# A fused attention and MLP kernel: a shorter attention pipeline, the first layer started one tick earlier, and the softmax multiply on another engine

## The chip, the cores and the metric

The kernel runs on one core of one Trainium2 chip. The metric is device microseconds (us) of one execution; the time before is the median of three runs. A core has TensorE (PE: matmuls and transposes, with PEld for its weight loads), VectorE (DVE), ScalarE (ACT), GpSimd (POOL) and SyncE (SP, which here issues most of the DMAs). Each engine works through its own queue in order, and semaphores order the engines among each other.

## The reference

Three parts follow one another on 2304 tokens of width 512:

```
scores = (q_c @ k_c.T) / sqrt(64)             # chunks of 64 tokens, 8 heads of 64
attn   = exp(scores - max); attn /= sum(attn) + 1e-9
x = attn @ v_c                                # 2304 x 512
h = relu(x @ w_in); x = (h * h) @ w_out       # 512 -> 2048 -> 512, w_in, w_out in float64
p = domain_probs / (sum + 1e-9)
out = sum over 4 experts of p[e] * (relu(x @ w1[e]) @ w2[e])   # 512 -> 1024 -> 512
```

## The kernel before

The 2304 tokens are 18 tiles of 128, two chunks of attention each. The first layer pair (`l1`: x @ w_in, `l2`: @ w_out) works on five blocks of 384, 384, 512, 512 and 512 tokens, in four passes over 512 hidden columns each; a step m is one pass, one block and one group of 128 hidden columns, 80 steps in all. Each step is 12 matmuls of `l1` (line 301) and 12 of `l2` (line 333) of the step before; each product is made of three, from a high and a low part of both operands.

The order of the work is written out by hand (`tc.manual_schedule()`): what the program text issues first stands first in its engine's queue. One loop runs over ticks r. In tick r the step of the first layer is m = r - LEAD. The first ticks also carry attention, one tile at several stages:

- `s0` of tile r+1: four transposes each of q and k (line 221), copied out of PSUM by ACT (line 225).
- `s1` of tile r: 32 small matmuls for the scores (line 236); DVE then takes the maximum and subtracts it (lines 242, 243).
- `exp` of tile r on ACT (line 249), `norm` of tile r-1 on DVE: sum, add, reciprocal (lines 254 to 256) and the multiply that normalises (line 257).
- `s2` of tile r-LAG_A: four transposes of the normalised scores (line 263), copied by ACT (line 265).
- `s3` of tile r-LAG_A: 32 small matmuls with v (line 277), written out as a high part by ACT (line 284) and a low part by DVE (line 285).

PE's queue in a tick of the attention is: `s1`, nine matmuls of `l1`, `s2`, `s0` of q, three of `l1` and three of `l2`, `s0` of k, three of `l2`, `s3`, the last six of `l2`. In ticks before LEAD the matmuls of the layers are absent. Between the matmuls of a step stand a relu on ACT (line 311), a squaring on DVE (line 312), and the split of the result (ACT line 316, DVE line 317).

The weights w_in and w_out arrive as 64-bit data and are converted on the way, one unit of 128x512 at a time: `unit_convert` is ACT (lines 128, 129), DVE (130, 133, and later in the tick 138, 141), and then POOL (142, 143); `unit_split` is ACT (154) and POOL (155). `FIRST` names the tick at which each of the first eight units is converted; it is loaded two ticks earlier and split one tick later. These are POOL's only instructions in the attention. SP issues at the start of tick r the loads of q and k of tile r+2, parts of v, and units of weights.

The scores of one tile live in `e`, of which there are LAG_A + 1 buffers. x of the first block is complete when `s3` of tile 2 is written out; the first `l1` reads it.

Of the kernel before, what the change touches and what calls it, by code (L numbers as in the profile page):

```python
# [13 lines left out]
ALU = mybir.AluOpType  # L14
# [4 lines left out]
P = 128  # L19
CH = 64  # L20
# [2 lines left out]
LAG = 1  # L23
RING_A = 4
RING_B = 4
LEAD = 5
QK_BUFS = 3
ACC_EARLY = 3
FIRST = [0, 1, 2, 3, 4, 5, 6, 7]
WARM = 8  # L30
SECOND = [-3, -2, -1, 1, 2, 3, 4, 5]
RAW_BUFS = 4
# [1 line left out]
HALF = 384  # L34
NSUP = 3
SWAP = 63
LAG_A = 2
UOFF = [1, 3, 5, 7, 9, 11, 13, 15]


# [5 lines left out]
def tile_kernel(ctx, tc, q, k, v, moe_w_in, moe_w_out, moe2_p, moe2_w1, moe2_w2, out):  # L46
    nc = tc.nc
    B, H, S, D = q.shape
# [5 lines left out]
    NTILE = NT // P  # L54
# [161 lines left out]
    def s0_stage(t, tags, which):  # L216
        nm, dst = (("q", qT), ("k", kT))[which]
        a = qkv.pop((nm, t))
        pt = bank(tags).rearrange("p (j s) -> p j s", j=HX)
        for j in range(HX):  # L220
            nc.tensor.transpose(  # L221
                out=pt[:, j, :], in_=a[:, 2 * j:2 * j + 2].rearrange("p x d -> p (x d)"), identity=ident
            )
        o = qkp.tile([P, HX, P], F32, tag=nm + "T", name=nm + "T")
        nc.scalar.copy(o, pt)
        dst[t] = o

    def s1_stage(t, tags):
        qt, kt = qT.pop(t), kT.pop(t)
        pt = [bank(tags)[:, :HX * CH].rearrange("p (j k) -> p j k", j=HX) for _ in range(2)]  # L230
        for c in range(2):
            cs = slice(c * CH, (c + 1) * CH)
            for j in range(HX):
                for x in range(2):
                    r = slice(x * CH, (x + 1) * CH)
                    nc.tensor.matmul(  # L236
                        pt[x][cs, j, :], lhsT=qt[r, j, cs], rhs=kt[r, j, cs], start=True, stop=True
                    )
        e = qkp.tile([P, HX, 2, CH], F32, tag="e", name="e", bufs=LAG_A + 1)
        mx = qkp.tile([P, 2, HX, 1], F32, tag="mx", name="mx")  # L240
        for x in range(2):
            nc.vector.tensor_reduce(out=mx[:, x], in_=pt[x], axis=AX.X, op=ALU.max)
            nc.vector.tensor_tensor(
                out=e[:, :, x, :], in0=pt[x], in1=mx[:, x].to_broadcast([P, HX, CH]), op=ALU.subtract
            )
        et[t] = e

    def exp_stage(t):
        nc.scalar.activation(out=et[t], in_=et[t], func=AF.Exp, scale=scale)

    def norm_stage(t):
        e = et[t].rearrange("p j x k -> p (j x) k")
        sm = qkp.tile([P, H, 1], F32, tag="sm", name="sm")
        nc.vector.tensor_reduce(out=sm, in_=e, axis=AX.X, op=ALU.add)
        nc.vector.tensor_scalar_add(sm, sm, 1e-9)
        nc.vector.reciprocal(sm, sm)
        nc.vector.tensor_tensor(out=e, in0=e, in1=sm.to_broadcast([P, H, CH]), op=ALU.mult)

    def s2_stage(t, tags):
        e = et.pop(t).rearrange("p j x k -> p j (x k)")  # L260
# [60 lines left out]
    def l2(i):  # L321
        p, tb, f = steps[i]
        T = BLOCKS[tb]
        bh, bl = halves[p * G + f, 1]
        hi, lo = gh.pop(i), gl.pop(i)
        for d in range(KD):
            ds = slice(d * P, (d + 1) * P)
            if f == 0:
                pacc[d] = bank("a")
            o = pacc[d][:, :T]  # L330
            prods = ((bh[:, ds], hi[:, :T]), (bh[:, ds], lo[:, :T]), (bl[:, ds], hi[:, :T]))
            for n, (w, y) in enumerate(prods):
                nc.tensor.matmul(  # L333
                    o, lhsT=w, rhs=y, start=(f == 0 and n == 0), stop=(f == G - 1 and n == 2)
                )
            if f == G - 1:
                evacuate(p, tb, d)
            yield
# [27 lines left out]
    for sp in range(NSUP):  # L366
        if sp < NSUP - 1:
            r = [starts[2 * sp] + i * P for i in range(3)] + [starts[2 * sp + 1] + i * P for i in range(3)]
        else:
            r = [starts[NB - 1] + i * P for i in range(3)] + [starts[2 + i] + HALF for i in range(3)]  # L370
# [200 lines left out]
    def at(tick, kind, fn, *args):  # L571
        jobs[kind].setdefault(max(0, tick), []).append((fn, args))

    def do(tick, kind):
        return [fn(*args) for fn, args in jobs[kind].pop(tick, ())]
# [11 lines left out]
    for p in range(npass1):  # L587
        for u, (f, which) in enumerate(order):
            if p == 0:
                tick = FIRST[u]  # L590
            elif p == 1:
                tick = NTILE + LAG_A + SECOND[u]
            else:
                tick = LEAD + (p - 1) * G * NB + UOFF[u]
            unit = (p * G + f, which)
            if tick > 1:
                at(tick - 2, "load", unit_load_later, *unit)
            at(tick, "convert", unit_convert, *unit)
            at(max(tick + 1, NTILE + LAG_A if p == 1 else 0), "split", unit_split, *unit)
    def run_all(loads):  # L600
        for y in loads:
            if hasattr(y, "__next__"):
                for _ in y:
                    pass

    with tc.manual_schedule():
# [27 lines left out]
        def mlp(m):  # L634
            if 0 <= m < NS:
                first = l1(m)
                for _ in range(KD):
                    yield next(first)
            second = l2(m - LAG) if 0 <= m - LAG else iter(((),) * KD)
            if r < NTILE + LAG_A:  # L640
                yield next(second)
            yield next(second)
            if 0 <= m < NS:
                for _ in first:
                    pass
            yield from second

        def run(chunks, n=None):
            while n is None or n > 0:
                try:  # L650
                    next(chunks)
                except StopIteration:
                    return
                n = None if n is None else n - 1
# [3 lines left out]
            SWAP: [(w1_load, (0,)), (w1_load, (1,)), (w2_load, (0,))],  # L658
            LEAD + NS - 4: [(w1_split, (0, 0)), (w1_split, (0, 1)), (w1_load, (2,))],
        }  # L660
        for i in range(4):
            early[SWAP + 5 + i] = [(w1_add, (0, i))]
            early[LEAD + NS - 8 + i] = [(w1_add, (1, i))]
        y0_at = LEAD + (npass1 - 1) * G * NB + 2 * G + LAG

        for which in range(2):
            s0_stage(0, "ttthaaaa", which)
        for r in range(LEAD + NS + LAG):
            m = r - LEAD
            tags = "ttthaaaa" if m < 0 else "t"  # L670
            ch = mlp(m) if m >= 0 else iter(())
            if r == NTILE + LAG_A:
                att.close()
                late["x"] = ctx.enter_context(tc.tile_pool(name="xq", bufs=1, side="right"))
                late["w"] = lw.enter_context(tc.tile_pool(name="wpb", bufs=RING_B, side="right"))
            run_all(do(r, "load"))
            if r < NTILE + LAG_A:
                if r < NTILE:
                    s1_stage(r, tags)
                if 0 <= r - 1 < NTILE:  # L680
                    norm_stage(r - 1)
                conv = do(r, "convert")
                for c in conv:
                    next(c)
                run(ch, 3)
                if 0 <= r - LAG_A:
                    s2_stage(r - LAG_A, tags)
                if r + 1 < NTILE:
                    s0_stage(r + 1, tags, 0)
                run(ch, 2)  # L690
                if r + 1 < NTILE:
                    s0_stage(r + 1, tags, 1)
                for c in conv:
                    run(c)
                run(ch, 1)
                if 0 <= r - LAG_A:
                    s3_stage(r - LAG_A, tags)
                if r < NTILE:
                    exp_stage(r)
                do(r, "split")  # L700
            else:
                if r == SWAP:
                    staging.close()
                    late["raw"] = ctx.enter_context(tc.tile_pool(name="raw", bufs=1, reuse_waits="tile"))
                for fn, args in early.pop(r, ()):
                    fn(*args)
                if r > y0_at:
                    next(late.setdefault("y0", y_combine(0)), None)
                if m < NS:
                    run(ch, KD + 2)  # L710
                    conv = do(r, "convert")
                    for c in conv:
                        next(c)
                    run(ch, 1)
                    for c in conv:
                        run(c)
                    do(r, "split")
            if m < NS:
                run(ch)
# [68 lines left out]
```

## Time and profile before

| what | us |
|---|---|
| median of 3 runs | 1249.46 (1248.11 to 1249.78) |
| span of the profiled execution, first to last instruction | 1246.2 |
| between span and median of the runs | 3.3 |
| PE busy | 1228.4 (99% of the span) |
| DVE busy | 687.5 (55%) |
| ACT busy | 522.7 (42%) |
| POOL busy | 621.7 (50%) |

The page gives the span of the profiled execution but no time of its own for it; the 3.3 us that the runs lie above the span are taken as what lies around it. In the page's strip of 40 slices of 31 us, PE stands at 7 and 8 tenths in the first two and at 9 or more in all others but the last; the granted TensorE clock (PEclk) is at 7 and 8 in the same two and at 9 after. Attention lasts until about 160 us of the span.

### The profile page before, as it was taken

What the parts mean: (1) busy time and instruction counts of PE and PEld (TensorE: products, weight loads), DVE (VectorE), ACT (ScalarE), POOL (GpSimd) and SP (SyncE); (2) the same over time, 40 slices, a digit from 0 to 9 for tenths busy, and PEclk for the clock granted to TensorE, in tenths of its full rate; (3) what the DMA queues carried; (4) which work ended last, traced back from release to release, by engine and by line L of the source; (5) the groups of instructions that cost most, each with busy time, mean ns of one, the idle gap of its engine ahead of it and who ended that gap; (6) DMA issues with size and microseconds to landing.
All of it is one profiled execution on the core that took longest, in us unless ns stands there. A gap on an engine that the chain in (4) does not pass through costs nothing.

```text
span 1246.2 us, 18128 instructions
## 1 busy us (share of the span) xinstructions
PE 1228.4 (99%) x7048; PEld 1088.0 (87%) x7048; DVE 687.5 (55%) x1135; ACT 522.7 (42%) x934; POOL 621.7 (50%) x507
## 2 busy tenths in 40 slices
PE   7899999999999999999999999999999999999998
PEld 6788889889889988888888888888888888888887
DVE  6966757555563445355555573555555735555555
ACT  5654555333432234533333355333333553333331
POOL 3510146421431023766766686767766866666650
PEclk7899999999999999999999999999999999999999
DMA  9855022210101000322222223222222132222211
GB/s 208 191 128 137 19 68 85 52 51 18 52 1 51 1 1 20 99 68 68 68 68 68 68 76 111 68 69 68 67 68 67 63 120 69 66 68 65 68 35 62
DMA packets 137253, 87.19 MB, mean 70 GB/s; under 512 B 63184, under 2 KB 120528, under 8 KB 137168
## 3 DMA queue, kind: packets, MB, share of 16 engines
q1 hardware_dynamic: 134544, 85.39, 25.1%
q8 instruction: 55, 0.90, 0.3%
q10 hardware_dynamic: 2624, 0.66, 0.3%
q14 instruction: 30, 0.25, 0.1%
HBM read 81.30 MB, written 4.72 MB: 69 GB/s over the span
## 4 chain that ended last, share of the span: by engine, by line
PE 94%; DVE 3%; DMA 1%; ACT 1%; issue 0%; SPq 0%; DVEq 0%; ACTq 0%
PE psa L548 32%; PE pst L503 24%; PE psa L333 15%; PE pst L301 9%; PE psh L301 6%; PE psh L503 4%; PE pst L277 1%; PE pst L221 1%; PE pst L236 1%; DMA q<-in_q 1%; DMA k<-in_k 1%; PE pst L263 0%; DVE cv L130 0%; DVE cv L133 0%; DVE cv L138 0%
## 5 line engine op out<-in xcount | busy, mean ns | idle before, releaser
L548 PE MATMUL psa<-ar 128*128 128x512 f32 x1728 | 445.7, 393 | 0.0
L548 PEld LDWEIGHTS psa<-ar 128*128 128x128 f32 x1728 | 320.0, 188 | 50.3
L471 POOL TENSOR_TENSOR ar<-raw,ar 128x896 fp32r<-128x896 f32 x96 | 204.1, 2128 | 274.7 <-ACT ar L470 274.7
L503 PE MATMUL pst<-ar 128*128 128x384 f32 x1728 | 339.2, 335 | 0.9 <-ACT u L512 0.9
L503 PEld LDWEIGHTS pst<-ar 128*128 128x128 f32 x1728 | 307.3, 188 | 22.9 <-ACT u L512 1.6
L561 DVE SCALAR_TENSOR_TENSOR o<-psa,prob,o 128x512 f32<-128x512 f32 x270 | 201.5, 748 | 173.4 <-PE psa L548 173.4
L142 POOL TENSOR_TENSOR raw<-raw 128x512 f32<-128x512 f32 x32 | 33.3, 1041 | 228.3 <-issue 103.9
L461 POOL TENSOR_TENSOR raw<-raw 128x256 f32<-128x256 f32 x192 | 140.4, 750 | 8.4 <-DMA raw<-in_moe_w 4.8
L480 POOL TENSOR_TENSOR ar<-raw,ar 128x512 fp32r<-128x512 f32 x96 | 123.4, 1305 | 12.5 <-ACT ar L479 12.5
L512 ACT COPY u<-pst 128x384 f32<-128x384 f32 x96 | 46.0, 479 | 163.7 <-PE pst L503 163.7
L333 PE MATMUL psa<-ar 128*128 128x512 f32 (+1 forms) x480 | 112.8, 375 | 0.1
L516 ACT ACTIVATE ar<-pst 128x384 fp32r<-128x384 f32 x96 | 47.2, 492 | 149.7 <-DVE pst L537 116.3
L333 PEld LDWEIGHTS psa<-ar 128*128 128x128 f32 x480 | 86.3, 188 | 12.6 <-DVE ar L317 0.4
L333 PE MATMUL psa<-ar,h 128*128 128x512 f32 (+1 forms) x320 | 93.2, 372 | 1.1 <-ACT ar L316 0.8
L516 ACT ACTIVATE ar<-psh 128x384 fp32r<-128x384 f32 x96 | 47.2, 492 | 109.8 <-DVE psh L526 78.6
L470 ACT CAST ar<-raw 128x896 fp32r<-128x896 f32 x96 | 90.0, 939 | 0.0
L517 DVE SCALAR_TENSOR_TENSOR ar<-psh,ar 128x384 fp32r<-128x384 f32 x96 | 53.5, 558 | 53.6 <-ACT ar L516 53.6
L317 DVE TENSOR_TENSOR ar<-r,ar 128x512 fp32r<-128x512 f32 (+1 forms) x80 | 60.6, 757 | 39.4 <-ACT ar L316 37.8
L517 DVE SCALAR_TENSOR_TENSOR ar<-pst,ar 128x384 fp32r<-128x384 f32 x96 | 53.5, 557 | 31.2 <-ACT ar L516 29.1
L312 DVE SCALAR_TENSOR_TENSOR r<-pst,r 128x512 f32<-128x512 f32 (+1 forms) x48 | 30.7, 640 | 71.2 <-ACT r L311 71.2
L311 ACT ACTIVATE r<-pst 128x512 f32<-128x512 f32 (+1 forms) x48 | 26.7, 557 | 102.8 <-PE pst L301 102.1
L301 PE MATMUL pst<-ar,h 128*128 128x512 f32 (+1 forms) x240 | 69.3, 370 | 0.0
(107 smaller groups left out, 1514.9 us busy)
## 6 DMA issues: line engine op xcount, KB each, us to landing
raw<-in_moe_w SPq DMA_DIRECT2D x48, 512.0 KB, 3.8
raw<-in_moe_w SPq DMA_DIRECT2D x48, 256.0 KB, 3.0
raw<-in_moe_w SPq DMA_DIRECT2D x96, 128.0 KB, 3.1
raw<-in_moe_w_in SPq DMA_DIRECT2D x16, 512.0 KB, 3.9
raw<-in_moe_w_out SPq DMA_DIRECT2D x16, 512.0 KB, 3.7
out<-o SPq DMA_DIRECT2D x18, 256.0 KB, 3.2
q<-in_q SPq DMA_DIRECT2D x16, 256.0 KB, 4.5
k<-in_k SPq DMA_DIRECT2D x14, 256.0 KB, 5.0
```

The costliest lines, as they stand in the source:

```text
L301: nc.tensor.matmul(ph[:, :T], lhsT=w[:, kk, :], rhs=x[tb][:, kk, :], start=(kk == 0 and n == 0), stop=(kk == KD - 1 and n == 2),)
L317: nc.vector.tensor_tensor(out=lo[:, :T], in0=r[:, :T], in1=hi[:, :T].bitcast(F32), op=ALU.subtract)
L333: nc.tensor.matmul(o, lhsT=w, rhs=y, start=(f == 0 and n == 0), stop=(f == G - 1 and n == 2))
L461: nc.gpsimd.tensor_tensor(out=r[:, o], in0=r[:, a], in1=r[:, b], op=op)
L470: nc.scalar.copy(h, a)
L471: nc.gpsimd.tensor_tensor(out=l, in0=a, in1=h.bitcast(F32), op=ALU.subtract)
L480: nc.gpsimd.tensor_tensor(out=l, in0=a, in1=h.bitcast(F32), op=ALU.subtract)
L503: nc.tensor.matmul(p, lhsT=w[:, kk, :], rhs=y[:, kk, :], start=(kk == 0 and z == 0 and u in (0, 1, 3)), stop=(kk == 1 and z == 2 and u in ...
L516: nc.scalar.activation(out=h, in_=p, func=AF.Relu)
L517: nc.vector.scalar_tensor_tensor(out=l, in0=p, scalar=0.0, in1=h.bitcast(F32), op0=ALU.max, op1=ALU.subtract)
L548: nc.tensor.matmul(p, lhsT=w[:, ts], rhs=y[:, i, :], start=(i == 0 and z == 0), stop=(i == 1 and z == 2))
L561: nc.vector.scalar_tensor_tensor(out=o, in0=p, scalar=pe, in1=o, op0=ALU.mult, op1=ALU.add)
```

## The change

Five things change together. `LEAD` goes from 5 to 4, so step m runs in tick m+4. `LAG_A` goes from 2 to 1, so `s2` and `s3` handle the tile of the tick before, and `e` has two buffers in place of three. `norm` of tile r-1 is issued ahead of `s1` of tile r, and `exp` of tile r after the first half of the conversion rather than after `s3`. The normalising multiply is issued to POOL. In `FIRST` the last two units are converted in ticks 5 and 6 in place of 6 and 7, so that tick 5 converts two units.

```diff
-LEAD = 5
+LEAD = 4
-FIRST = [0, 1, 2, 3, 4, 5, 6, 7]
+FIRST = [0, 1, 2, 3, 4, 5, 5, 6]
-LAG_A = 2
+LAG_A = 1
@@ norm_stage
-        nc.vector.tensor_tensor(out=e, in0=e, in1=sm.to_broadcast([P, H, CH]), op=ALU.mult)
+        nc.gpsimd.tensor_tensor(out=e, in0=e, in1=sm.to_broadcast([P, H, CH]), op=ALU.mult)
@@ the loop over ticks, r < NTILE + LAG_A
+                if 0 <= r - 1 < NTILE:
+                    norm_stage(r - 1)
                 if r < NTILE:
                     s1_stage(r, tags)
-                if 0 <= r - 1 < NTILE:
-                    norm_stage(r - 1)
                 conv = do(r, "convert")
                 for c in conv:
                     next(c)
+                if r < NTILE:
+                    exp_stage(r)
                 run(ch, 3)
                 if 0 <= r - LAG_A:
                     s2_stage(r - LAG_A, tags)
...
                     s3_stage(r - LAG_A, tags)
-                if r < NTILE:
-                    exp_stage(r)
                 do(r, "split")
```

## Rows read from the trace of the kernel before

**Rows 1.** Windows: start:end, length, busy us (instructions) by engine, granted clock, DMA share, GB/s

```profile
10.00:20.00 10.00, 8.04 (x84) 6.22 (x84) 7.98 (x20) 6.78 (x12) 3.37 (x3) 0.50 1.17 222
30.00:40.00 10.00, 6.73 (x91) 5.67 (x87) 9.59 (x21) 6.38 (x13) 4.76 (x5) 0.66 0.99 219
40.00:50.00 10.00, 9.34 (x113) 8.53 (x113) 9.47 (x21) 7.30 (x14) 6.16 (x5) 1.00 0.86 205
```

**Rows 2.** Timeline of PE, 27 to 75 us: start, us, line, what [idle before, releaser]

```profile
27.88 0.63 PE L221 MATMUL psa<-ident,k 128*128 128x128 f32 x4 [0.69 <-DMA k<-in_k]
...
34.69 1.12 PE L221 MATMUL pst<-ident,k 128*128 128x128 f32 x4 [1.49 <-DMA k<-in_k]
...
39.23 2.19 PE L301 MATMUL psh<-ar 128*128 128x384 f32 x9 [0.17 <-DVE ar L285]
41.26 0.60 PE L263 MATMUL pst<-ident,e 128*128 128x128 f32 x4
...
46.91 0.60 PE L263 MATMUL pst<-ident,e 128*128 128x128 f32 x4
...
55.70 0.60 PE L263 MATMUL pst<-ident,e 128*128 128x128 f32 x4
...
63.64 0.60 PE L263 MATMUL pst<-ident,e 128*128 128x128 f32 x4
...
71.76 0.60 PE L263 MATMUL pst<-ident,e 128*128 128x128 f32 x4
```

**Rows 3.** Chain that ended last, 74 to 81 us: start, us, what

```profile
74.98 1.08 PE pst L277 x32
76.05 1.27 PE psa L333 x6
77.32 0.91 PE pst L236 x30
78.23 1.78 PE psh L301 x9
80.01 0.44 PE pst L263 x4
```

**Rows 4.** Timeline of POOL, 13 to 48 us

```profile
13.06 1.29 POOL L143 TENSOR_TENSOR cv<-cv,raw 128x512 f32<-128x512 f32 x1
...
41.09 1.29 POOL L155 TENSOR_TENSOR ar<-cv,ar 128x512 fp32r<-128x512 f32 x1
45.83 1.04 POOL L142 TENSOR_TENSOR raw<-raw 128x512 f32<-128x512 f32 x1 [3.45 <-ACT e L249]
46.95 1.48 POOL L143 TENSOR_TENSOR cv<-cv,raw 128x512 f32<-128x512 f32 x1
```

**Rows 5.** Timeline of DVE, 41 to 78 us

```profile
41.39 1.02 DVE L255 TENSOR_SCALAR sm<-sm 128x8 f32<-128x8 f32 x1
...
48.78 0.68 DVE L254 TENSOR_REDUCE sm<-e 128x8 f32<-128x512 f32 x1
...
49.98 0.69 DVE L257 TENSOR_TENSOR e<-e,sm 128x512 f32<-128x512 f32 x1
...
58.75 0.55 DVE L312 SCALAR_TENSOR_TENSOR r<-psh,r 128x384 f32<-128x384 f32 x1
59.22 0.68 DVE L138 SCALAR_TENSOR_TENSOR cv<-raw,cv 128x512 int32<-128x512 int32 x1
59.93 0.43 DVE L141 TENSOR_SCALAR raw<-cv 128x512 int32<-128x512 int32 x1
...
61.95 1.38 DVE L317 TENSOR_TENSOR ar<-r,ar 128x384 fp32r<-128x384 f32 x1 [0.75 <-ACT ar L316]
...
76.72 0.69 DVE L285 TENSOR_TENSOR ar<-pst,ar 128x512 fp32r<-128x512 f32 x1 [1.48 <-ACT ar L284]
77.65 0.56 DVE L317 TENSOR_TENSOR ar<-r,ar 128x384 fp32r<-128x384 f32 x1 [0.24 <-ACT ar L316]
```

**Rows 6.** Timeline of SP's queue, 34 to 42 us

```profile
34.60 7.41 SPq L199 DMA_DIRECT2D v<-in_v  x8
```

## The prediction

> **What bounds the kernel now.** I read the page's busy table first: PE is busy 1228.4 of 1246.2 us, so a microsecond can only be won where PE waits or runs slowly. The strip of 40 slices puts nearly all of that into the first 40 us, and the windows confirm it: 6.73 of 10 us busy with a mean granted clock of 0.66 between 30 and 40, 0.50 throughout between 10 and 20 (the lower of the two levels, 1.2 GHz), and 9.34 at clock 1.00 from 40 on [rows 1]. Then I read PE's timeline for the waits. Up to 39.23 PE runs attention alone, and the first `l1` starts there, released by DVE's line 285 of tile 2 [rows 2]. That tile was late because k of tile 5, which stands ahead of `s3` of tile 2 in PE's queue, landed only at 34.69 [rows 2]. From 39.23 on PE is bound by its own work: `s2` follows `s2` after 5.65 (the first tick, which has no `l2`), 8.79, 7.94 and 8.12 us [rows 2]; the chain shows the pieces of such a tick without a gap [rows 3]. DVE is nearly as full (9.59 and 9.47 of 10) [rows 1]; POOL has room on average (4.76 and 6.16), but what matters is when it is free.
>
> **What the change moves.** PE's work stays what it was. The first `l1` needs attention up to tile 2 and, with one tick less, one tile of `s0` and `s1` less ahead of it. That tile has to be done later, behind the first layer, and costs there 0.88 for eight transposes (twice the 0.44 of four) and 0.91 for its scores [rows 3]: 1.8. So a first `l1` that starts d earlier wins d - 1.8.
>
> The other side: `s2` of tile r-1 now stands in tick r, behind nine `l1` matmuls, and needs a multiply issued in the same tick. PE works in order, so everything behind `s2` waits with it: `s0`, the rest of `l1`, `l2`, `s3`. In POOL's queue that multiply stands behind all that the tick before issued there: lines 142, 143 and 155. Before, POOL's work was needed only ticks later; now its end is on PE's path.
>
> **Price of the multiply.** The trace has no multiply by a broadcast operand on POOL. DVE's took 0.69 [rows 5]. On POOL the same 128x512 elements took 1.04 (line 142, a multiply on strided operands) and 1.29 (lines 143, 155) [rows 4]. I take 1.3, since its operand `e` lies contiguous as theirs do; the low end is 1.04, the high end 1.48, line 143 beside a busy DVE [rows 4].
>
> **Start.** `s2` of tile 0 waits in tick 1 for POOL: line 143 ends at 14.35 [rows 4], so 14.35 + 1.3 + 0.05 = 15.7. From there each of three ticks is a loop. At the high clock it is set by POOL: DVE finishes the scores' max about when `s2` starts, then converts (four instructions, 2.1), then POOL does 1.1 + 1.25 + 1.3 + 1.3 with handovers: 7.2. At the low clock it is set by PE: `s2`, `s0` and `s3` about 4.3, lines 284 and 285 1.3, the sum 0.7 and then line 255 behind POOL's split, and the multiply: about 9. PE still idles between the bursts as it does now, so I take the middle, 8.1: `s2` of tile 3 at 15.7 + 3 x 8.1 = 40.0, against 41.26 [rows 2]. Less the 1.8 owed, the start costs 0.5 us; with 7.2 throughout it wins 2.1, with 9.0 it costs 3.2.
>
> **Ticks with weight units (r = 4 to 7).** From one `s2` to the next through POOL: `s2`, `s0` of q and three `l1` 1.4 [rows 3], relu on ACT taken as long as line 312, 0.55, with handovers 2.1 in all; then line 312 to 138 0.47, to 141 0.71, its 0.43 and a handover 0.55 [rows 5]; lines 142, 143, 155 on POOL 1.12, 1.26, 1.28 [rows 4]; the multiply 1.3 and a handover: 8.85.
> - r = 4 (one conversion, one split): 8.85 for 5.65, 3.2 lost.
> - r = 5 (two conversions, one split): 1.12 + 1.26 more, 11.2 for 8.79, 2.4 lost.
> - r = 6 (one conversion, two splits): 10.1 for 7.94, 2.2 lost.
> - r = 7 (one split): here the way is by lines 284, 154, 316, 317 and the three norm instructions; `s3`'s end to multiply's end 4.8 for PE's 3.97 (1.27 + 0.91 + 1.78 [rows 3]): 8.7 for 8.12, 0.6 lost.
> The sum is 8.4. What hides it now is the whole tick by which `s2` lagged.
>
> **Ticks without units.** Line 285 starts 76.72; line 317 follows at 77.3 (the exp no longer stands between), the norm at 77.8; its three instructions take 1.2 (48.78 to 49.98), the multiply ends at about 80.4, and `s2` would be due at 80.01 [rows 3, 5]. 0.3 to 0.4 in each of three ticks, r = 8 to 10: 1.1. With 512 columns in `l1` from r = 12 on, PE has half a microsecond more and nothing is lost, except in r = 16 and 17, which convert a unit again: 0.5 and 1.0 by the same chain without a split. 1.5.
>
> **DVE against POOL.** Line 255, a tiny instruction, lasted 1.02 from 41.39, until POOL's line 155 ended at 42.38; line 317 took 1.38 beside line 143 and 0.56 alone [rows 4, 5]. Now both stand on the way to the multiply, in ticks whose POOL queue is full. Where they meet POOL's instructions each time, the four ticks lose a further 0.4, 0.9, 0.65 and 0.8, 2.75 together; where they slip between two of them, nothing. I take half, 1.4.
> The Trainium skill (SBUF — State Buffer, "Who interferes with whom") says that VectorE and GpSimd share one port pair as a lock for a whole instruction; the 1.02 and 1.38 agree. By it every meeting blocks, and the sum would be 1.4 higher. The same notes (Perfetto Trace Analysis, "Optimizing Scalar/DVE Operations") say that offloading between the two might therefore not help. None of the rows shows more than single meetings.
>
> **Everything else.** The multiply gone from DVE (0.69 a tick) is worth nothing once PE is the bound. The loads: one unit moves ahead of q and k of tile 6, about 0.6 us of SP and 512 KB; as PE is no earlier than before, they still land in time. Two buffers of `e` suffice, since `s2` of r-2 is over before `s1` of r writes. After tick 19 the queues hold what they held.
>
> **Sum.** 0.5 + 8.4 + 1.1 + 1.5 + 1.4 = 12.9. On the span of 1246.2 that gives 1259.1; with the 3.3 around it, 1262.4, and I predict 1262, 12.5 over the median shown. The low end of the multiply (1.04, nine ticks, -2.3), the quick start (-2.6) and no meetings (-1.4) give 1256; the slow start (+2.7), all meetings (+1.4) and 1.48 (+1.6) give 1268.
>
> **Rivals.**
> *The start decides, faster.* If the early loop isn't set by POOL, the first `l1` starts when k of tile 4 allows: 27.88 [rows 2] + 0.45 + `s3` 1.08 + lines 284, 285 1.3 = 30.8, which is 8.4 earlier and wins 6.6. PE is then early for the loads: SP spends 7.41 from 34.60 on the next v [rows 6], with one more unit ahead of it, and `s3` of tile 4 waits some 2 us; the ticks without units cost 1.1. That gives 1246. It decides if POOL's waits after the start stay below 4 us. For it: before, DVE was busy 9.6 of 10 us there and is relieved of 0.69 a tick. Against: POOL's order, and units in every early tick. 0.13.
> *The two cancel.* The ticks overlap better than I chain them, the start wins 3 to 4 and the waits cost the same: 1249.5. 0.08.
> *The clock falls as well, slower still.* PE now idles 2.4 to 3.6 us in ticks 4 to 6. Before 40 us the idle between bursts went with clock 0.50 and 0.66 [rows 1], and nine `l1` matmuls took 2.19 where 1.78 is their usual [rows 2, 3]. Two ticks at the low level cost 2.5 to 3 each: 1268. Against: the ticks before were emptier. 0.17.
> The forecast itself, 1255 to 1266, has 0.62.
>
> **Chances.** 0.2% (2.5 us) is about what a measurement tells from no change. Faster: 0.11, nearly all of the first rival. Same: 0.02 of it and 0.06 of the second, 0.08. Slower: 0.62 + 0.17 + 0.02 = 0.81. The range for 8 in 10 is 1251 to 1270: below it lies the first rival and part of the second, above it the worst of the third.
>
> **What would show it.** Right: PE's waits in 38 to 80 us end on POOL's write of `e` at line 263, longest in the ticks that convert two units or split two; POOL's line 257 starts right behind line 155; the first `l1` at 35 to 38. Wrong: line 263 waits for nothing, or `l1` starts at 31 and the waits name DMAs. A PE clock below 1.00 between 40 and 70 would be the third rival.

## The result and the profile after

The changed kernel takes 1263.80 us (median of four runs, 1259.72 to 1263.99); before it was 1248.88 on the same chips. The ratio is 1.0112, 95% interval 1.0100 to 1.0123: slower, by 15 us by the medians and 14 by the ratio, which is taken over all runs, where 12.5 was forecast. The profiled execution spans 1262.0 us against 1246.2, 15.8 more. PE is busy for the same time (1228.6 against 1228.4), so on balance all of it is idle time of PE. Within that balance a higher clock ahead of the first `l1` (mean granted clock 0.86, before 0.75) makes PE busy for less time, and a lower clock in two later ticks for more.

The waits of PE in the attention (engine, output, line, what it waited for: us in total, times, longest):

```profile
PE pst L263 <- POOL e L257: 15.9, 11, 3.7
PE psa L263 <- POOL e L257: 6.2, 2, 3.2
...
PE psa L221 <- DMA q<-in_q: 0.7, 1, 0.7
```

22.1 us of waiting stand at line 263, `s2`, for line 257, the normalising multiply that is now on POOL. Before, no wait of PE named either; the DMA waits at line 221, of which [rows 2] shows two, are all but gone, because PE now comes later than the loads.

PE's timeline, 36 to 92 us; the last field is the idle time before and its releaser:

```profile
36.75 1.66 PE L301 MATMUL psh<-ar 128*128 128x384 f32 x8 [0.23 <-DVE ar L285]
39.77 0.66 PE L263 MATMUL pst<-ident,e 128*128 128x128 f32 x4 [1.35 <-POOL e L257]
...
48.66 1.11 PE L263 MATMUL pst<-ident,e 128*128 128x128 f32 x4 [3.24 <-POOL e L257]
...
61.89 1.11 PE L263 MATMUL pst<-ident,e 128*128 128x128 f32 x4 [3.73 <-POOL e L257]
...
73.94 0.66 PE L263 MATMUL pst<-ident,e 128*128 128x128 f32 x4 [1.53 <-POOL e L257]
...
83.34 0.65 PE L263 MATMUL pst<-ident,e 128*128 128x128 f32 x4 [1.28 <-POOL e L257]
...
91.65 0.66 PE L263 MATMUL pst<-ident,e 128*128 128x128 f32 x4 [0.19 <-POOL e L257]
```

Read the starts as differences. The first `s2` beside the first layer comes 1.5 us earlier than in [rows 2] (39.77 for 41.26), with a tile's `s0` and `s1`, 1.8 us, still owed. From there `s2` follows `s2` after 8.89, 13.23, 12.05, 9.40 and 8.31 us; the first four stand against 5.65, 8.79, 7.94 and 8.12 in [rows 2], the fifth against the 7.9 of a full tick. The two groups of four transposes that take 1.11 in place of 0.66 ran at the lower clock: the granted clock is 0.50 from 48.66 to 50 and from 61.89 to 65.

POOL's timeline in the tick with two conversions and the next one:

```profile
53.96 1.36 POOL L142 TENSOR_TENSOR raw<-raw 128x512 f32<-128x512 f32 x1 [5.35 <-ACT kT L225]
55.40 1.36 POOL L143 TENSOR_TENSOR cv<-cv,raw 128x512 f32<-128x512 f32 x1
56.73 1.35 POOL L142 TENSOR_TENSOR raw<-raw 128x512 f32<-128x512 f32 x1
58.16 1.27 POOL L143 TENSOR_TENSOR cv<-cv,raw 128x512 f32<-128x512 f32 x1
59.39 1.26 POOL L155 TENSOR_TENSOR ar<-cv,ar 128x512 fp32r<-128x512 f32 x1
60.62 1.22 POOL L257 TENSOR_TENSOR e<-e,sm 128x512 f32<-128x512 f32 x1
...
69.58 2.85 POOL L155 TENSOR_TENSOR ar<-cv,ar 128x512 fp32r<-128x512 f32 x2
72.84 1.04 POOL L257 TENSOR_TENSOR e<-e,sm 128x512 f32<-128x512 f32 x1 [0.41 <-DVE sm L256]
```

Line 257 starts where line 155 ends, behind five instructions of weight conversion without a gap; PE's `s2` at 61.89 is released 0.05 after its end. The multiply takes 1.22 here and 1.04 in the next tick. There POOL's queue is no longer what comes last: POOL idles 0.41 before the multiply, for DVE's reciprocal (line 256).

DVE's timeline, its meetings with POOL:

```profile
45.85 0.55 DVE L255 TENSOR_SCALAR sm<-sm 128x8 f32<-128x8 f32 x1
...
54.45 1.15 DVE L141 TENSOR_SCALAR raw<-cv 128x512 int32<-128x512 int32 x1
...
69.75 1.52 DVE L317 TENSOR_TENSOR ar<-r,ar 128x384 fp32r<-128x384 f32 x1 [0.76 <-ACT ar L316]
```

They take 0.17, 0.43 and 0.56 where POOL is idle. Line 317 ends at 71.27; the norm comes after it and the multiply after the norm.

### The profile page after: what moved, and what is told of

Same layout as the page of the kernel before. It is cut to its first block, busy times and chain, and to the rows that moved or that the text cites. A ratio compares the mean times of both kernels' runs of the same rounds, so it can differ in the third digit from the quotient of the medians.

```text
span 1262.0 us, 18170 instructions
## 1 busy us (share of the span) xinstructions
PE 1228.6 (97%) x7048; PEld 1088.4 (86%) x7048; DVE 674.4 (53%) x1117; ACT 522.2 (41%) x934; POOL 641.0 (51%) x525
## 4 chain that ended last, share of the span: by engine, by line
PE 84%; DVE 2%; ACT 1%; issue 0%; DVEq 0%
PE psa L548 32%; PE pst L503 24%; PE psa L333 12%; PE pst L301 9%; PE psh L503 4%; PE psh L301 3%; DVE cv L130 0%; DVE ar L317 0%; DVE cv L133 0%; DVE r L312 0%; ACT ar L316 0%; DVE cv L138 0%; DVE acc L350 0%; ACT r L311 0%; PE pst L277 0%
## 5 line engine op out<-in xcount | busy, mean ns | idle before, releaser
L480 POOL TENSOR_TENSOR ar<-raw,ar 128x512 fp32r<-128x512 f32 x96 | 123.4, 1306 | 12.5 <-ACT ar L479 12.5
```

Of the source, the lines that this page charges most:

```text
L480: nc.gpsimd.tensor_tensor(out=l, in0=a, in1=h.bitcast(F32), op=ALU.subtract)
```

## The experiments

Times are medians, each with its ratio to the kernel before, timed beside it on the same chip. The ratios are taken over all runs, so differences by ratios and by medians can be 2 us apart.

**The multiply back on DVE.**

```diff
-        nc.gpsimd.tensor_tensor(out=e, in0=e, in1=sm.to_broadcast([P, H, CH]), op=ALU.mult)
+        nc.vector.tensor_tensor(out=e, in0=e, in1=sm.to_broadcast([P, H, CH]), op=ALU.mult)
```

> The changed kernel with the normalising multiply back on DVE; all else as changed. Theory (the multiply waits for its turn in POOL's queue, behind lines 142, 143 and 155): in the ticks with weight units the way from s2 to s2 gets shorter, not short, because DVE's lines 317, 255 and 257 still meet POOL: about 8.6 in place of 8.9, 10.3 for 13.2, 10.2 for 12.1, 8.7 for 9.4, and 7.95 for 8.3 in the three ticks without units; some 2 us at the start. In all 10 less: 1254. Rival (s2 asked for in the same tick is late whoever multiplies): only the 1.04 - 0.69 of each multiply comes back, 13 ticks, 4.5: 1259.

Measured 1264.03, ratio 1.0123 (1.0108 to 1.0139): no time came back, and both expectations were wrong. From `s2` to `s2` it takes 9.92, 11.42, 11.13 and 10.22 us where the changed kernel has 8.89, 13.23, 12.05 and 9.40: two ticks are shorter, two longer. Rows of PE, ACT, POOL and DVE from the first of these ticks:

```profile
40.34 0.66 PE L263 MATMUL pst<-ident,e 128*128 128x128 f32 x4 [0.50 <-DVE e L257]
41.96 0.64 ACT L249 ACTIVATE e<-e 128x512 f32<-128x512 f32 x1 [2.91 <-DVE e L243]
43.44 0.50 ACT L311 ACTIVATE r<-psh 128x384 f32<-128x384 f32 x1
...
48.30 1.26 POOL L155 TENSOR_TENSOR ar<-cv,ar 128x512 fp32r<-128x512 f32 x1
...
48.64 1.47 DVE L257 TENSOR_TENSOR e<-e,sm 128x512 f32<-128x512 f32 x1
...
50.26 0.63 PE L263 MATMUL pst<-ident,e 128*128 128x128 f32 x4 [3.04 <-DVE e L257]
```

and ACT's rows of the same tick in the changed kernel, where `s2` starts at 39.77:

```profile
39.45 0.63 ACT L249 ACTIVATE e<-e 128x512 f32<-128x512 f32 x1 [1.82 <-DVE e L243]
...
41.47 0.51 ACT L311 ACTIVATE r<-psh 128x384 f32<-128x384 f32 x1
```

Two things keep the tick long. First, the multiply on DVE takes 1.47 where 0.69 is usual: it ends at 50.11, 0.55 after POOL's line 155 (49.56), and only then does `s2` start. So it still comes behind POOL's work, though it is no longer in POOL's queue; in the next two ticks it takes 1.62 and 1.50. Second, the multiply now stands in DVE's queue ahead of the scores' max and subtract (lines 242, 243). ACT's exp waits for line 243 and, in the changed order, stands ahead of ACT's copies and of the relu. So the relu (line 311) starts 3.10 after `s2`, where the changed kernel has 1.70, and what follows the relu on DVE and POOL comes 1.4 later. The second part is the larger one in this tick (1.4 against 0.8); it is read from these rows, no run tested it alone.

In ticks without units no wait stands at line 263, but a tick still takes 8.24 (91.31 to 99.55), no better than 8.31: `s0` of q starts at 92.06, 0.75 behind `s2`, where the changed kernel has 0.50 (91.65 to 92.15), and DVE, with a longer norm in front, ends its reading of the scores' banks at 91.95 and 92.74. That `s0` waits for the first of them is argued from the times; no row names it.

**The norm in its own tick.**

```diff
-                if 0 <= r - 1 < NTILE:
-                    norm_stage(r - 1)
                 if r < NTILE:
                     s1_stage(r, tags)
...
                 if r < NTILE:
                     exp_stage(r)
+                    norm_stage(r)
```

> The changed kernel with the norm of tile r issued in tick r, right behind its exp, and so ahead of that tick's lines 142, 143 and 155 in POOL's queue; the multiply stays on POOL, the lag stays one tick. Theory (place in POOL's queue): the waits of line 263 for line 257 vanish, the loop at the start is no longer POOL's, the first l1 starts at 31 to 34 when k of tile 4 and s3 of tile 2 allow, then some waits for loads: 1243 to 1250, 1246. Rival (a lag of one tick, or POOL's multiply itself, is too slow): line 263 still waits, over 1257.

Measured 1250.84, ratio 1.0023 (1.0013 to 1.0033): 13 of the 15 us gone by the medians, 11 of 14 by the ratios, with one call moved; the time lies just above the expected 1243 to 1250. The first matmul of `l1` starts at 31.45; the other eight wait for line 285 until 33.68 (36.07 and 36.75 in the changed kernel). But `s2` to `s2` takes 10.5 and 13.2 around the tick with two conversions. Its largest waits:

```profile
PE pst L221 <- issue: 2.3, 2, 1.2
PE psa L221 <- DMA q<-in_q: 2.1, 2, 1.3
PE pst L221 <- DMA k<-in_k: 2.0, 2, 1.2
PE psh L301 <- DVE ar L285: 1.8, 1, 1.8
PE pst L263 <- DVE ar L285: 1.5, 2, 1.1
```

Loads and DVE have taken over, besides waits at line 221 for which the profile shows no releaser ("issue"), and the granted clock is 0.50 from 54 to 58. Line 263 waits for line 257 twice, 2.0 us, both before the first layer. The rival that a lag of one tick or POOL's multiply is too slow falls.

**The kernel before with the multiply on POOL.** Line 257 alone is edited, as above in reverse.

> The kernel before with nothing but the multiply moved to POOL; lag of two ticks, first layer in tick 5. Theory: s2 comes a whole tick later, so the same POOL queue hides it, no wait of line 263 for line 257; 1249, within 2. Rival (the multiply on POOL costs by itself, by blocking DVE's lines 130, 133, 255 and 317): 0.5 to 1 us in each of 15 ticks, 1255 or more.

Measured 1247.65, ratio 0.9994 (0.9985 to 1.0003): no change, as the theory had it. With two ticks of lag the same multiply behind the same queue is hidden.

**Without the low words of the first pass.**

```diff
-        nc.gpsimd.tensor_tensor(out=lf, in0=hi.bitcast(F32), in1=lf, op=ALU.mult)
-        nc.gpsimd.tensor_tensor(out=af, in0=af, in1=lf, op=ALU.add)
+        if n >= G:
+            nc.gpsimd.tensor_tensor(out=lf, in0=hi.bitcast(F32), in1=lf, op=ALU.mult)
+            nc.gpsimd.tensor_tensor(out=af, in0=af, in1=lf, op=ALU.add)
```

> The changed kernel without lines 142 and 143 for the units of the first pass (their low 32-bit words are left out of the weights), so POOL has only the split and the multiply there. Theory: s2 to s2 falls to the way by lines 317 and the norm: 7.3 for 8.9 (r = 4), 8.7 for 13.2, 9.4 for 12.1, and 1 us at the start, 9 to 10 less: 1254. Rival (DVE's own chain or ACT's order holds the norm back, not POOL's queue): less than 3 us less, over 1260.

Measured 1255.97, ratio 1.0060 (1.0045 to 1.0075): the theory's size, but spread otherwise. `s2` of tile 3 comes at 36.14, 3.6 earlier than in the changed kernel; the intervals after it are 8.38, 11.05, 9.80 and 9.43, of 8.89, 13.23, 12.05 and 9.40. POOL's timeline there (its lines are one further):

```profile
51.56 1.29 POOL L156 TENSOR_TENSOR ar<-cv,ar 128x512 fp32r<-128x512 f32 x1 [7.10 <-ACT ar L155]
54.47 1.04 POOL L258 TENSOR_TENSOR e<-e,sm 128x512 f32<-128x512 f32 x1 [1.62 <-DVE sm L257]
```

POOL now idles 1.62 before the multiply, for DVE's reciprocal. So there are two queues to the same effect: with POOL emptied, the norm is late on DVE, which issues it behind the tick before's lines 285 and 317. The 11.05 also has a stretch at the lower clock in it (0.50 from 46 to 47, behind a wait of 2.67). The rival was partly right.

**Idle matmuls in the wait.**

```diff
                 run(ch, 3)
+                if 5 <= r <= 6:
+                    fill = bank("t")
+                    for _ in range(6):     # 13 in the second run
+                        nc.tensor.matmul(fill[:, :P], lhsT=ident, rhs=ident, start=True, stop=True)
                 if 0 <= r - LAG_A:
```

> The changed kernel with six idle matmuls (identity by identity, 0.47 us each at the high clock, result unused) ahead of s2 in ticks 5 and 6, where PE waits 3.2 and 3.7 us and comes back at clock 0.50. Theory (the low clock after the waits costs 1.4 and 1.6 us, as s2 to s3 takes 4.4 and 4.6 there and 3.0 at the high clock): the two intervals fall from 13.2 and 12.1 to about 11.9 and 10.6; 1261. Rival (POOL's queue sets the next s2 anyhow, PE's speed is hidden): no change, 1263 to 1264.

Measured 1262.31, ratio 1.0106 (1.0092 to 1.0120). It tested nothing: six matmuls took 1.5 us, not 2.8, two microseconds of idle were left, and the clock fell to 0.50 as before.

> The changed kernel with thirteen idle matmuls (identity by identity, result unused) ahead of s2 in ticks 5 and 6. Six of them took only 1.5 us of PE, two microseconds of wait were left and the clock fell all the same, so that run did not test it; thirteen should take 3.25 us, about the whole wait. Theory (the low clock after the wait costs 1.4 and 1.6 us): the clock stays at 1.00 in ticks 5 and 6, s2 to s3 takes 3.0 in place of 4.4 and 4.6, s2 to s2 falls to about 12 and 10.7; 1261. Rival (POOL's queue sets the next s2 anyhow): clock at 1.00 and no change, 1263 to 1264.

Measured 1261.56, ratio 1.0102 (1.0085 to 1.0119). Windows of the changed kernel (start:end, length, busy by engine, granted clock, DMA share, GB/s):

```profile
48.00:51.00 3.00, 2.34 (x10) 2.34 (x11) 2.07 (x5) 1.55 (x3) 0.60 (x1) 0.53 1.11 294
61.00:65.00 4.00, 3.11 (x13) 3.11 (x14) 1.12 (x1) 1.25 (x3) 0.84 (x1) 0.60 0.14 31
```

and the same stretches with thirteen idle matmuls:

```profile
48.00:51.00 3.00, 2.49 (x22) 2.30 (x22) 2.79 (x8) 1.10 (x2) 1.78 (x2) 1.00 1.32 232
61.00:65.00 4.00, 3.21 (x25) 2.92 (x27) 1.99 (x3) 2.09 (x4) 0.74 (x1) 1.00 0.22 51
```

PE's timeline of that run, its `s2`:

```profile
49.84 0.66 PE L263 MATMUL pst<-ident,e 128*128 128x128 f32 x4 [0.51 <-POOL e L257]
...
61.79 0.65 PE L263 MATMUL pst<-ident,e 128*128 128x128 f32 x4 [0.94 <-POOL e L257]
...
72.09 0.65 PE L263 MATMUL pst<-ident,e 128*128 128x128 f32 x4 [0.76 <-POOL e L257]
```

The clock stays at 1.00, and the two intervals are 11.95 and 10.30 for 13.23 and 12.05: 3.0 us, the sum the theory named. In the times 2.2 of it shows by the medians and 1.2 by the ratios; its profile gave 0.9 back at the start, where the clock was low for a while from 33 us. The intervals of the total (1.0085 to 1.0119 and 1.0100 to 1.0123) overlap; the clock's price rests on these rows of one profile each. That the idle matmuls are what kept the clock up is likely but not shown beyond doubt: in the next run it stayed at 1.00 behind a wait of 3.37 without any.

**One tick of lag, but the first layer in tick 5 and one unit per tick.**

```diff
-LEAD = 4
+LEAD = 5
-FIRST = [0, 1, 2, 3, 4, 5, 5, 6]
+FIRST = [0, 1, 2, 3, 4, 5, 6, 7]
```

> The changed kernel with the first layer in tick 5 again and one unit per tick (LEAD 5, FIRST as before); the lag of one tick, the order of norm and exp and the multiply on POOL stay. Theory (norm behind the tick's unit work is what costs): s2 still waits in each tick with a unit, 8.9 for the first, 9.3 for the next ones, the start loses some 4 and the no-unit and late ticks 2 to 3: 1261. Rival (the two-unit tick and the earlier first layer are what costs): 1250 to 1254.

Measured 1262.75, ratio 1.0099 (1.0083 to 1.0116). The time is the theory's, but more of it than expected lies at the start: the first `l1` starts at 46.71, 7.5 later than in the kernel before, since each tick ahead of it waits for the late norm: line 263 waits for line 257 at 15.37, 23.80, 32.53 and 40.71, for 1.82 to 3.25. From there `s2` follows `s2` after 9.13, 9.50, 9.70 and 9.38. So the earlier layer and the crowded tick aren't what costs; the lag with the norm's place is. Rows of PE behind its longest wait, all at the higher clock (1.00 from 50 to 66):

```profile
58.59 0.66 PE L263 MATMUL pst<-ident,e 128*128 128x128 f32 x4 [3.37 <-POOL e L257]
...
59.44 0.77 PE L301 MATMUL psh<-ar 128*128 128x384 f32 x3
```

**The norm in its own tick, first layer in tick 5.** Both edits, of the run with the norm in its own tick and of the last one.

> Norm issued in its own tick (as in the run with the norm in the same tick, 1250.8), with LEAD 5 and FIRST as before. That run still waited for loads and for DVE's line 285 around its two-unit tick and lost some 3 us to the low clock. Theory (what was left there comes from the crowded ticks 5 and 6): with one unit per tick and the loads a tick ahead the waits go, the later start costs no more than they did: 1246 to 1249. Rival (DVE is the bound of these ticks however they are spread): 1250 to 1252.

Measured 1246.44, ratio 0.9986 (0.9977 to 0.9994): the only kernel here that beats the one before, by 1.8 us (0.14%, with the interval's end close below 1). Against the run before this one in the list (1262.75) the one moved call is worth 16.3 by the medians, 14 by the ratios. PE's timeline, from an execution of 1248.17, one of the three longest of eleven:

```profile
42.14 0.60 PE L263 MATMUL pst<-ident,e 128*128 128x128 f32 x4
...
48.77 0.63 PE L263 MATMUL pst<-ident,e 128*128 128x128 f32 x4 [0.59 <-DVE ar L285]
...
59.61 0.60 PE L263 MATMUL pst<-ident,e 128*128 128x128 f32 x4
67.54 0.60 PE L263 MATMUL pst<-ident,e 128*128 128x128 f32 x4
```

After the first layer has started, no `s2` waits for the multiply; from 59.61 on a tick is 7.93. The longest tick left is 10.8 (48.77 to 59.61); the granted clock is 0.50 from 51 to 53 in it.

**The norm in its own tick, multiply on DVE, LEAD 4.**

> Norm issued in its own tick, LEAD 4, with the multiply on DVE. Theory (place in the tick decides, not the engine): within 1.5 us of the same kernel with the multiply on POOL, 1249.5 to 1252. DVE has 0.6 more a tick but line 138 is no longer held up by POOL's multiply (1.42 for 0.68). Rival (the engine decides): DVE falls behind, 1254 or more; or POOL's lock was the rest, 1247 or less.

Measured 1253.18, ratio 1.0030 (1.0020 to 1.0039). Beside the same kernel with the multiply on POOL (1.0023, 1.0013 to 1.0033) it is 0.9 us slower by the ratios, 2.3 by the medians, and the intervals overlap. The time lies between the two ranges expected. The norm's place decides 13 us with the multiply on POOL (1263.80 to 1250.84) and 11 with it on DVE (1264.03 to 1253.18); which engine is better stays open.

## Why the prediction was right

*Bound and start.* PE is bound by its own work, so only its waits count: right. `s2` of tile 3 was forecast at 40.0 from three loops of 8.1; it came at 39.77 (loops of 8.67, 8.13 and 7.21). That the start is a loop through the late norm and not k's arrival is shown by the norm in its own tick, which starts `l1` at 31.45, near the first rival's 30.8. That POOL alone sets this loop isn't shown: with the multiply on DVE `s2` of tile 3 comes no earlier (40.34), while without lines 142 and 143 it comes 3.6 earlier (36.14).

*Ticks with units.* Forecast without and with every meeting on the port, and found: r = 4: 8.85 to 9.25, 8.89. r = 5: 11.2 to 12.1, 13.23. r = 6: 10.1 to 10.75, 12.05. r = 7: 8.7 to 9.5, 9.40. With the clock held up, r = 5 and 6 came to 11.95 and 10.30, inside the bounds, and the four ticks lose 10.0 where 8.4 + 1.4 was forecast. The half taken for the meetings was too little in r = 5 and 7, where nearly all of them happened: the rule of the Trainium skill (SBUF — State Buffer, "Who interferes with whom") was the better guide, and line 317's 1.52 and line 141's 1.15 in the rows above agree with it.

*Ticks without units and late ticks.* A loss of 0.3 to 0.4 was forecast for each; a tick takes 8.31, 0.38 more than the 7.93 of a tick without a wait; in r = 16 and 17 waits of 0.22 and 1.03 at line 263 for the 0.5 and 1.0 forecast.

*The multiply.* The step that was mis-sized: 1.3 was taken, 1.04 measured in nearly all ticks (1.22 at most), the low end, as line 142, the other multiply. It is about 2 us over the nine ticks. (A smaller slip: 1.27 + 0.91 + 1.78 is 3.96, not 3.97.)

*The clock.* The third rival came true beside the forecast, smaller than priced: the clock fell in ticks 5 and 6 and cost 1.3 and 1.75 by the intervals, 3 together, not 5 to 6. One of its signs was misread: 2.19 for nine `l1` matmuls is a row of the timeline and 1.78 one of the chain; in the timeline the usual is 1.85. Sum of forecast and clock, 12.9 + 3.0, is 15.9; the spans differ by 15.8. The price of the multiply and the meetings of DVE and POOL, one too high and the other too low, cancelled in it. The median is nearer still, 1263.8 for 1262, but that is luck: the 3.3 taken as what lies around the span was 1.8 here (1263.80 less 1262.0).

*What the prediction did not see.* For r = 4 to 6 it named POOL's queue as the cause. That holds for r = 4 and 5, where line 257 starts as line 155 ends. In r = 6 POOL idles 0.41 before the multiply, for DVE, which is late through line 317's 1.52. Asking for the norm at the head of the tick puts it behind everything that the tick before still has on DVE and on POOL, and the run with the multiply on DVE shows that another engine alone doesn't get round this: there the multiply is held up by POOL's line 155 all the same, and itself holds up the max, the exp and the relu.

That two kernels with the same lag differ by 14 to 16 us through the norm's place, and that the kernel before hides the multiply on POOL for nothing, is shown. How much of the remaining long tick in the best kernel is loads, PSUM banks or clock was not tested.

## What to carry to other kernels

When a pipeline loses a stage of slack, price every queue ahead of the instruction that is now due, on each engine that it passes, not its own duration: here 1.04 us of multiply came with up to five POOL instructions ahead of it. Issue the short work that the critical engine waits for before the long work that it doesn't, and ask only then which engine should do it. Where one engine's instructions hold up another's, as line 155 did the multiply on DVE, price the two queues together. And look at what the moved instruction now stands ahead of on its new engine.

## What the runs showed that I had not expected

The kernel takes the same with the late multiply on DVE as on POOL (1264.03 and 1263.80): beside POOL's instructions 0.69 became 1.47, and the max, the exp and the relu came later.

PE's clock fell to half behind waits of 3.24 and 3.73 us, behind one of 2.67 in the run without the low words, and behind one of 2.08 with six idle matmuls ahead of it. It did not fall behind waits of 1.35 and 1.53, but neither did it behind 3.25 (at 32.56 in the changed kernel, 1.00 from 30 to 38) or 3.37 (first layer in tick 5). So the length of the wait alone doesn't tell here whether the clock falls. With 3 us of idle matmuls in each of the two long waits it stayed up. Six identity matmuls in float32 took 1.5 us of PE.
